# Unread products ahead of the first Gram matrix and ahead of N, and where chunk 0's and 1's K K^T lies

## The chip, the cores and the metric

The kernel runs on one core of a Trainium2 chip. The metric is the device time of one execution in microseconds (us). The engines are named as in the profile: PE (TensorE, the matrix products), PEld (its weight loads), DVE (VectorE), ACT (ScalarE), POOL (GpSimd) and SP (SyncE, which issues most transfers). Each has its own instruction stream and runs it in order; they meet at semaphores. All data are float32.

## The reference

The first half is a delta rule over 32 pairs of batch and head (4 batches, 8 heads, sequence 768, head size 48). For every step t, with k normalised:

```
y[t]  = q[t] @ state
v_old = k[t] @ state
state = state + beta[t] * outer(k[t], v[t] - v_old)
```

Its output, laid out as 3072 tokens by 384, goes through a feed-forward block with an inner size of 1536:

```
g   = x @ w_gate
out = (g * sigmoid(g) * (x @ w_val)) @ w_out
```

## The kernel before

The sequence is cut into 12 chunks of 64 steps. Inside a chunk the recurrence is solved in matrix form: K K^T of the chunk (the Gram matrix), a triangular inverse built from it and from beta, and products with v, q and the state. The 16 slots of a partition are ordered by `par`, the parity of the head, and by two more indices; a batch half and a parity decide which 64 partitions a block uses. The feed-forward block works on 256 tokens, those of one chunk, at a time.

Chunks 0 and 1 are prepared in a stage of their own, in the first 35 us. The functions that matter:

- `load_k`, `load_q`, `load_v` (L133 to L184) issue the first transfers, on SP and ACT.
- `norms(c)` (L361) computes the norms of k on DVE.
- `unread` (L633) issues 94 products of 32 x 32 with one column, whose result nothing reads. They write the PSUM tile `px` and stand at the head of PE's stream.
- `turned(c, of_q, tag)` (L473) transposes k or q of a chunk on PE, eight blocks of 128 x 128 (L497), and ACT copies them to SBUF (L499 or L501). The tag says where in PSUM: a number names two of the four banks `ffn0` to `ffn3`, a string one of the pairs of banks `px` and `py`.
- `first_gram(c, tag)` (L646) forms the Gram matrix of chunk 0 or 1 in 64 products of 32 columns by 64 or by 2 x 32 (L656, L657). Chunk 0 uses the pair `px`, chunk 1 the pair `py`; one tile holds both parities.
- `first_diag(c, p)` (L660) copies the diagonal 32 x 32 blocks to `mb`, in one ACT instruction of 128 x 512.
- `first_n` (L447) turns norms into their reciprocals on DVE (L449, L451, L453); `first_scale` (L673) multiplies beta by them on POOL (L677 to L679) and scales the diagonals on DVE (L682). Between them DVE transposes the diagonals (L1649).
- `low_copies(c, p)` (L664) copies three strips of 16 columns below the diagonal to `l_sb`, one ACT instruction of 128 x 256 each (L667).
- `first_substitution` (L686) inverts the diagonal blocks on DVE (L698, L704), `first_z` transposes the result (L708) and `spread_z` (L711) writes it out twice on ACT and DVE (L717, L719). This is z.
- `warm(3)` (L640) issues three products of 128 columns by 512 (L644), again unread, in `px`.
- `n_products` (L721) forms N from the strips and z (L728). Then `advance(0)` multiplies z with v (L938) and adds three products with N (L958).

The engines' order is written out by hand: inside `manual_schedule` every engine gets its instructions in program order (L1620 to L1706), so what stands earlier in the text is earlier in each engine's queue. Around the change PE's order is: unread products, transposes and Gram matrix of k of chunk 0, transposes of k of chunk 1, beta's products (L438), Gram matrix of chunk 1, transposes of q of chunk 0 and k of chunk 2, q's product of chunk 0 (L513, banks 2 and 3), transposes of k of chunk 3 and q of chunk 1, the Gram matrices of chunks 2 and 3 (L513, `px` and `py`), q's product of chunk 1, the three long products, N.

After that PE works through the feed-forward products and the remaining chunks, interleaved, until the end (L1708 to L1749).

Of the kernel before, what the change touches and what calls it, by code (L numbers as in the profile page):

```python
# [15 lines left out]
R = 32  # L16
# [4 lines left out]
def kernel(  # L21
# [25 lines left out]
    nc = tc.nc  # L47
# [21 lines left out]
    def ps_pair(name, tag):  # L69

        return psum.tile([128, 2, 512], FP32, name=name, tag=tag, bufs=1)
# [7 lines left out]
    def ps_ffn(shape, name, bank=None):  # L79
        if bank is None:  # L80
            taken.append(name)
            bank = (len(taken) - 1) % 4
        n = 1
        for m in shape[1:]:
            n *= m
        p = ffn_banks[bank][:, 0:n]
        return p if len(shape) == 2 else p.rearrange("p (x n) -> p x n", x=shape[1])
# [54 lines left out]
    def load_k(c, dmas=(nc.sync,)):  # L142
        load_heads(kn_of(c), k, c, dmas)

    def load_q(c):
        load_heads(qpad[c % QB], q, c)
# [163 lines left out]
    half = const.tile([128, R], FP32, name="half")  # L310
# [20 lines left out]
    m_low = const.tile([128, 3], FP32, name="m_low")  # L331
# [14 lines left out]
    def half_of(x):  # L346
        return slice(64 * x, 64 * x + 64)

    def every():
        for bp in range(NB):  # L350
            for j in range(NJ):
                for n, (par, b) in enumerate(ORDER):
                    yield bp, j, par, b, bp == 0 and j == 0
# [3 lines left out]
    def new_n(g):  # L357

        n_t[g] = work.tile([128, 2, HH], FP32, name="n_t")
# [106 lines left out]
    def banks(name, tag):  # L466

        if type(tag) is int:
            return [ps_ffn([128, 512], name, tag + i) for i in range(2)]
        p = ps_pair(name, tag)  # L470
        return [p[:, 0], p[:, 1]]
# [75 lines left out]
    def gram(*args):  # L547
        for _ in gram_steps(*args):
            pass
# [51 lines left out]
    B16 = R // 2  # L601
# [28 lines left out]
        )  # L630
        nc.vector.tensor_scalar_mul(m_low, m_rows[:, 0:3], -1.0)

    def unread():  # L633

        p = ps_pair("p_t", "px")[:, 0]
        for n in range(94):
            q_ = QUADS[n % 4][0]
            nc.tensor.matmul(p[q_, 0:1], half[q_], half[q_, 0:1])

    def warm(count):  # L640

        p = ps_pair("p_t", "px")[:, 0]
        for _ in range(count):
            nc.tensor.matmul(p, ident, kts[0][:, 0:512])  # L644

    def first_gram(c, tag):  # L646

        p_g = ps_pair("p_g", tag)
        p_v = p_g.rearrange("p par (x h i) -> p par x h i", x=2, i=R)
        half_rows = C  # L650
        for bp, j, par, b, _ in every():
            k_v = kt[c][half_of(par), bp, j, b].rearrange("p (x i) -> p x i", x=2)
            h, s_ = NJ * bp + j, b ^ par
            hi, lo = slice(64 * s_, 64 * s_ + R), slice(64 * s_ + R, 64 * s_ + C)
            twice = k_v[:, 0:1].to_broadcast([half_rows, 2, R])
            nc.tensor.matmul(p_v[hi, par, :, h], k_v[:, 0], twice)  # L656
            nc.tensor.matmul(p_v[lo, par, :, h], k_v[:, 1], k_v)  # L657
        return p_v

    def first_diag(c, p):  # L660
        to = first_of["diag"][:, HH * c : HH * c + HH]
        nc.scalar.copy(to.rearrange("p (par h) j -> p par h j", par=2), p[:, :, 1])

    def low_copies(c, p):  # L664
        l_v = l_sb[c].rearrange("p (par h) k -> p par h k", par=2)
        for x in range(3):
            nc.scalar.mul(  # L667
                l_v[:, :, :, B16 * x : B16 * x + B16],
                p[:, :, x // 2, :, B16 * (x % 2) : B16 * (x % 2) + B16],
                m_low[:, x : x + 1],  # L670
            )

    def first_scale(r_b):  # L673
        zb, b = first_of["zb"], beta_b[:, 0]
# [418 lines left out]
    def units(t):  # L1093
        return t.rearrange("p (u n) -> p u n", u=4)
# [74 lines left out]
    p_x, p_w, p_y, p_v = (units(bank) for bank in ffn_banks)  # L1169
# [328 lines left out]
    def steps(kind, *args):  # L1498
        return gens.get((kind, args), (None, 0))[1]
# [120 lines left out]
    with tc.manual_schedule(  # L1620
        engines={
            mybir.EngineType.PE,
            mybir.EngineType.Activation,
            mybir.EngineType.DVE,
            mybir.EngineType.SP,
            mybir.EngineType.Pool,
        }
    ):
        new_n(0)
        load_beta()  # L1630
        first_tiles()
        norms(0)
        norms(1)
        load_q(0)
        load_k(2)
        load_k(3)
        load_q(1)
        load_v(0)
        copy_a = nc.scalar.copy
        unread()  # L1640
        turned(0, False, 0)
        p_g = [first_gram(0, "px")]
        first_diag(0, p_g[0])
        turned(1, False, 2)
        spread_beta(copy_a)
        p_g.append(first_gram(1, "py"))
        first_diag(1, p_g[1])
        r_b = first_n()
        nc.vector.transpose(first_of["mb"][:, 0 : R * R], first_of["flat"])  # L1649
        first_scale(r_b)  # L1650
        for n in range(12):
            stage(n, n - 2 if n > 1 else None)
        load_v(1)
        stage(12, 10)
        stage(13, 11)
        low_copies(0, p_g[0])
        turned(0, True, 0)
        low_copies(1, p_g[1])
        turned(2, False, "px")
        first_q = [gram_steps(0, True, 2)]  # L1660
        next(first_q[0])
        turned(3, False, "py")
        turned(1, True, 0)
        gram(2, False, "px", (copy_a, copy_a))
        gram(3, False, "py", (copy_a, copy_a))
        first_q.append(gram_steps(1, True, 0))
        next(first_q[1])
        for n in (0, 2):
            power_step(n)
        first_substitution()  # L1670
        for n in range(14, 18):
            stage(n, n - 3)
        first_z()
        for n in range(18, 23):
            stage(n, n - 3)
        some, others = slice(0, HH // 2), slice(HH // 2, HH)
        spread_z(0, 1, nc.scalar, some)
        spread_z(0, 0, nc.vector)
        spread_z(0, 1, nc.vector, others)
        scale_v(0)  # L1680
        for steps_of in first_q:
            next(steps_of)
        warm(3)
        new_nt(0, qpad[1].rearrange("p bp h d -> p (bp h d)"))
        zb_1 = work.tile([128, R, R], FP32, name="zb", bufs=1)
        new_nt(1, zb_1.rearrange("p k i -> p (k i)"))
        step("advance", advance, 0)
        for x in range(2):
            spread_z(1, x, nc.scalar)
        for n in (4, 1, 3, 5, 6, 7):  # L1690
            power_step(n)
        for _ in range(6):
            step("advance", advance, 0)
        converts_first(0)
        step("advance", advance, 0)
        converts_first(2)
        p_n = banks("p_n", "px")
        n_products(1, p_n, (0,))
        step("advance", advance, 0)
        converts_first(4)  # L1700
        n_products(1, p_n, (1,))
        converts_first(1, 3)
        converts_first(5)
        scale_v(1)
        for par in range(2):
            n_copy(1, p_n, par)  # L1706

        def chain(at):  # L1708

            step("advance", advance, 0 if steps("advance", 0) < 4 else 1)  # L1710
            converts(1 + (at + 1) % 2)

        pairs = [(c, f) for c in range(2) for f in range(0, 8, 2)]
        pairs += [(c, f) for f in range(8, FT, 2) for c in range(2)]
        for at, (c, f) in enumerate(pairs):
            early = c == 0 and f < 4
            if c == 1 and f == 0:
                finish(1)
                second_inverse.append(invert(1))
                for _ in range(3):  # L1720
                    next(second_inverse[0])
            elif not early:
                point(2)
            need((6, 12, 18, 24, 30, 30)[f // 2])
            gate_val(c, f, fill, at, chain if early else None)
        need(len(pieces))
        for bp in range(NB):
            point(2)
            output(0, bp, fill, (4, 8))
        output(1, 0, fill, (4, 8))  # L1730
        hold.clear()
        first_blocks(True)
        first_blocks(False)
        point(2)
        output(1, 1, fill, range(2, FT, 2))
        finish(2)
        x_sums(2)
        sums_of_w(12)
        for c in range(2, NCH):
            if c > FAST:  # L1740
                begin(c, 0)
            point(c + 1)
            if c == FAST:
                begin(c, 0)
            for r in range(ROUNDS):
                gate_val_fast(c, r, fill)
            output_fast(c, fill)
            finish(c + 1)
            x_sums(c + 1)  # L1749
# [30 lines left out]
```

## Time and profile before

| what | value |
|---|---|
| median of three runs | 702.68 us (701.88, 702.68, 706.95) |
| profiled execution | 704.07 us, of which the span of the profile is 702.4 us |
| mean granted clock of PE over the span | 0.994 |
| PE busy | 97% of the span, 11450 product records |
| DVE, ACT, POOL busy | 67%, 37%, 8% |
| chain that ended last | PE 95%, ACT 2%, issue 1%, DVE 1%, DMA 1% |

How to read the profile: an instruction is named by its line in the kernel, its engine and its operation, with the tiles it writes and reads. A float32 product leaves two records on PE and two weight loads on PEld. A wait is put down to the engine or transfer whose semaphore came last; "issue" means that the engine waited for nothing that the profile shows. The start of a record is counted from the start of the span.

### The profile page before, as it was taken

What the parts mean: (1) busy time and instruction counts of PE and PEld (TensorE: products, weight loads), DVE (VectorE), ACT (ScalarE), POOL (GpSimd) and SP (SyncE); (2) the same over time, 40 slices, a digit from 0 to 9 for tenths busy, and PEclk for the clock granted to TensorE, in tenths of its full rate; (3) what the DMA queues carried; (4) which work ended last, traced back from release to release, by engine and by line L of the source; (5) the groups of instructions that cost most, each with busy time, mean ns of one, the idle gap of its engine ahead of it and who ended that gap; (6) DMA issues with size and microseconds to landing.
All of it is one profiled execution on the core that took longest, in us unless ns stands there. A gap on an engine that the chain in (4) does not pass through costs nothing.

```text
span 702.4 us, 25797 instructions
## 1 busy us (share of the span) xinstructions
PE 684.1 (97%) x11450; PEld 643.0 (92%) x11450; DVE 473.0 (67%) x1103; ACT 259.4 (37%) x542; POOL 54.0 (8%) x62
## 2 busy tenths in 40 slices
PE   6899999999999999999999999999999999999997
PEld 5788888757999989999999999999999999999997
DVE  6786788798899738887468787379844345333342
ACT  4674865214442523244223235232153132142220
POOL 4110031105000120000300000200000000000000
PEclk9999999999999999999999999999999999999999
DMA  8578724017450621365333264143241131221210
GB/s 133 155 183 210 215 85 141 4 37 174 126 108 13 118 69 46 77 130 91 75 84 72 56 133 88 31 117 84 55 107 48 42 84 59 55 62 46 68 46 23
DMA packets 143855, 62.33 MB, mean 89 GB/s; under 512 B 122976, under 2 KB 126048, under 8 KB 143744
## 3 DMA queue, kind: packets, MB, share of 16 engines
q1 hardware_dynamic: 141536, 60.19, 36.3%
q8 instruction: 90, 1.47, 0.8%
q10 hardware_dynamic: 2080, 0.39, 0.4%
q0 software_dynamic: 128, 0.10, 0.1%
q14 instruction: 21, 0.17, 0.1%
HBM read 53.58 MB, written 7.08 MB: 86 GB/s over the span
## 4 chain that ended last, share of the span: by engine, by line
PE 95%; ACT 2%; issue 1%; DVE 1%; DMA 1%; ACTq 0%; DVEq 0%
PE ffn L1174 43%; PE ffn L1380 20%; PE ffn L1270 9%; PE ffn L1297 4%; PE p_g L513 3%; PE p_u L938 2%; PE p_r L899 2%; PE p_s L1006 2%; PE p_y L908 2%; PE p_y L994 1%; PE p_f L1067 1%; PE p_u L958 1%; PE ffn L958 1%; PE ffn L497 1%; PE p_j L876 1%
## 5 line engine op out<-in xcount | busy, mean ns | idle before, releaser
L1174 PE MATMUL ffn<-x_ffn,wg_sb 128*128 128x128 f32 x840 | 128.9, 276 | 0.4 <-ACT x_ffn L1073 0.2
L1174 PE MATMUL ffn<-x_ffn,wv_sb 128*128 128x128 f32 x840 | 128.5, 276 | 0.0
L1174 PEld LDWEIGHTS ffn<-x_ffn,wg_sb 128*128 128x128 f32 x840 | 111.7, 193 | 0.6 <-ACT ffn L1230 0.3
L1174 PEld LDWEIGHTS ffn<-x_ffn,wv_sb 128*128 128x128 f32 x840 | 111.1, 193 | 0.1
L1204 ACT ACTIVATE sil<-ffn 128x256 f32<-128x256 f32 x120 | 46.1, 384 | 133.6 <-PE ffn L1174 125.3
L1380 PE MATMUL ffn<-wo_sb,h_f 128*128 128x192 f32 x480 | 83.4, 327 | 0.0
L1209 DVE TENSOR_TENSOR h_f<-sil,ffn 128x256 f32<-128x256 f32 x120 | 49.6, 418 | 49.5 <-ACT sil L1204 47.2
L1380 PEld LDWEIGHTS ffn<-wo_sb,h_f 128*128 128x128 f32 x480 | 78.1, 190 | 0.4
L1341 DVE TENSOR_TENSOR ffn<-ffn,p_sb 128x512 f32<-128x512 f32 x58 | 40.3, 695 | 44.3 <-ACT ffn L1230 43.2
L1174 PE MATMUL ffn<-x_t,h_f 128*128 128x128 f32 x480 | 61.0, 280 | 0.2 <-ACT ffn L1187 0.2
L1174 PEld LDWEIGHTS ffn<-x_t,h_f 128*128 128x128 f32 x480 | 56.2, 191 | 1.4 <-ACT ffn L1187 0.4
L591 DVE TENSOR_TENSOR zb<-zb,tmp 128x31 f32<-128x31 f32 (+15 forms) x155 | 53.1, 343 | 5.3
L585 DVE TENSOR_TENSOR tmp<-zb,mb 128x31 f32<-128x31 f32 (+15 forms) x155 | 52.7, 340 | 4.0
L807 POOL TENSOR_TENSOR n_b<-mb,half 128x32 f32<-128x32 f32 x5 | 30.0, 6003 | 294.6 <-DVE mb L555 294.6
L1341 DVE TENSOR_TENSOR o_sb<-o_sb,ffn 128x192 f32<-128x192 f32 x49 | 17.2, 352 | 51.2 <-PE ffn L1380 49.1
L1187 ACT COPY ffn<-ffn 128x512 f32<-128x512 f32 x30 | 17.1, 571 | 63.7 <-PE ffn L1174 57.3
L1380 PE MATMUL ffn<-last_k,h_f 128*128 128x192 f32 x200 | 35.9, 327 | 0.0
L1270 PE MATMUL ffn<-x_ffn,wg_sb 128*128 128x256 f32 x144 | 34.4, 385 | 0.0
L1270 PE MATMUL ffn<-x_ffn,wv_sb 128*128 128x256 f32 x144 | 33.8, 382 | 0.0
L1380 PEld LDWEIGHTS ffn<-last_k,h_f 128*128 128x128 f32 x200 | 32.9, 190 | 0.0
L1174 PE MATMUL ffn<-x_ffn,p_sb 128*128 128x128 f32 x216 | 30.9, 287 | 0.0
L1270 PEld LDWEIGHTS ffn<-x_ffn,wg_sb 128*128 128x128 f32 x144 | 26.5, 190 | 4.4 <-DVE wg_sb L304 0.8
(289 smaller groups left out, 1070.0 us busy)
## 6 DMA issues: line engine op xcount, KB each, us to landing
h_f<-w_s SPq DMA_DIRECT2D x60, 256.0 KB, 2.7
p_sb<-w_s SPq DMA_DIRECT2D x27, 256.0 KB, 2.9
vin<-in_v_dram SPq DMA_DIRECT2D x48, 96.0 KB, 3.0
out_dram<-o_sb SPq DMA_DIRECT2D x48, 96.0 KB, 2.2
kn<-in_k_dram SPq DMA_DIRECT2D x20, 192.0 KB, 4.8
zt<-in_moe_w_out_dram SPq DMA_DIRECT2D x6, 384.0 KB, 3.7
qpad<-in_q_dram SPq DMA_DIRECT2D x36, 64.0 KB, 2.9
w_s<-h_f SPq DMA_DIRECT2D x7, 256.0 KB, 4.3
```

Of the source, the lines that this page charges most:

```text
L513: nc.tensor.matmul(p_v[par][half_of(b if of_q else b ^ par), bp, j], kt[c][half_of(par), bp, j, b], xt[half_of(par), bp, j, b],)
L585: nc.vector.tensor_tensor(out=t_v, in0=zb[:, 0 : j + 1, j : j + 1].to_broadcast([128, j + 1, m]), in1=mb[:, j : j + 1, j + 1 : R].to_broad ...
L591: nc.vector.tensor_tensor(out=zb[:, 0 : j + 1, j + 1 : R], in0=zb[:, 0 : j + 1, j + 1 : R], in1=t_v, op=ALU.add,)
L807: nc.gpsimd.tensor_tensor(out=n, in0=mb.rearrange("p j i -> p (j i)")[:, 0 : R * R : R + 1], in1=half, op=ALU.pow,)
L1174: nc.tensor.matmul(p[:, u], w(u), moving, start=start and u == 0, stop=True, skip_group_check=True,)
L1187: nc.scalar.copy(p_y, p_x)
L1204: nc.scalar.activation(sil[:, n].rearrange("p (i n) -> p i n", i=2), p[:, 0:2], ACTF.Silu)
L1209: nc.vector.tensor_tensor(out=h_of(c, f, j), in0=sil[:, n].rearrange("p (i n) -> p i n", i=2), in1=p[:, 2:4], op=ALU.mult,)
L1270: nc.tensor.matmul(ps[name][:, i], w_sb[:, t, (f + i) * 128 : (f + i + 1) * 128], xts[c][:, t], start=(t == 0 and i == 0), stop=(t == KT - 1),
L1297: nc.tensor.matmul(p_o, hs[c, f - f % 2][:, f % 2, bp * 128 : (bp + 1) * 128], wo_sb[:, f], start=(f == 0), stop=(f == FT - 1),)
L1341: nc.vector.tensor_tensor(out=out, in0=a, in1=b, op=ALU.add)
L1380: nc.tensor.matmul(p[x, part], a(f - f % 2)[:, f % 2], b(f), start=not begun and f == 0, stop=f == FH - 1, skip_group_check=True,)
```

## The change

It has three parts, all in the stage of chunks 0 and 1.

First, the unread products. `unread` now issues five products of 32 columns by 512 (the moving operand is one column repeated) in place of 94 small ones. The small products have a function of their own, and 56 of them stand ahead of N, where one long product of `warm` is left of three.

Second, the Gram matrices of chunks 0 and 1 have a tile for each parity (`banks`). For chunk 0 these are the two halves of `px`, as before; chunk 1 moves from `py` to the banks `ffn2` and `ffn3`, in which its k was transposed just before.

Third, the copies out of them. The diagonals are copied by parity: for chunk 0 both on ACT, for chunk 1 one on ACT and one on DVE. DVE's copy stands ahead of `first_n` in DVE's order. `low_copies` issues six ACT instructions of 128 x 128 instead of three of 128 x 256.

```diff
-    def unread():
+    def unread(count):
 
         p = ps_pair("p_t", "px")[:, 0]
-        for n in range(94):
+        for _ in range(count):
+            nc.tensor.matmul(p[0:R], half, half[:, 0:1].to_broadcast([128, 512]))
+
+    def small_unread(count):
+
+        p = ps_pair("p_t", "px")[:, 0]
+        for n in range(count):
             q_ = QUADS[n % 4][0]
             nc.tensor.matmul(p[q_, 0:1], half[q_], half[q_, 0:1])
...
     def first_gram(c, tag):
 
-        p_g = ps_pair("p_g", tag)
-        p_v = p_g.rearrange("p par (x h i) -> p par x h i", x=2, i=R)
+        p_v = [p.rearrange("p (x h i) -> p x h i", x=2, i=R) for p in banks("p_g", tag)]
...
-            nc.tensor.matmul(p_v[hi, par, :, h], k_v[:, 0], twice)
-            nc.tensor.matmul(p_v[lo, par, :, h], k_v[:, 1], k_v)
+            nc.tensor.matmul(p_v[par][hi, :, h], k_v[:, 0], twice)
+            nc.tensor.matmul(p_v[par][lo, :, h], k_v[:, 1], k_v)
         return p_v
 
     def first_diag(c, p):
         to = first_of["diag"][:, HH * c : HH * c + HH]
-        nc.scalar.copy(to.rearrange("p (par h) j -> p par h j", par=2), p[:, :, 1])
+        to = to.rearrange("p (par h) j -> p par h j", par=2)
+        nc.scalar.copy(to[:, 0], p[0][:, 1])
+        if c == 0:
+            nc.scalar.copy(to[:, 1], p[1][:, 1])
+        else:
+            nc.vector.tensor_copy(to[:, 1], p[1][:, 1])
 
     def low_copies(c, p):
         l_v = l_sb[c].rearrange("p (par h) k -> p par h k", par=2)
-        for x in range(3):
-            nc.scalar.mul(
-                l_v[:, :, :, B16 * x : B16 * x + B16],
-                p[:, :, x // 2, :, B16 * (x % 2) : B16 * (x % 2) + B16],
-                m_low[:, x : x + 1],
-            )
+        for par in range(2):
+            for x in range(3):
+                nc.scalar.mul(
+                    l_v[:, par, :, B16 * x : B16 * x + B16],
+                    p[par][:, x // 2, :, B16 * (x % 2) : B16 * (x % 2) + B16],
+                    m_low[:, x : x + 1],
+                )
...
-        unread()
+        unread(5)
...
-        p_g.append(first_gram(1, "py"))
+        p_g.append(first_gram(1, 2))
...
-        warm(3)
+        small_unread(56)
+        warm(1)
```

## The prediction

> **What bounds the kernel now.** I read the engine totals first, then PE's list of waits, then the timelines of PE, ACT and DVE over the first 36 us, where all of the change lies, and last the groups of the transposes.
>
> ```profile
> PE 684.1 (97%) x11450; PEld 643.0 (92%) x11450; DVE 473.0 (67%) x1103; ACT 259.4 (37%) x542; POOL 54.0 (8%) x62
> ...
> q8 instruction: 90, 1.47, 0.8%
> ```
> ```profile
> PE ffn L497 <- DVE wo_sb L1649: 2.6, 1, 2.6
> PE p_j L876 <- issue: 2.4, 2, 1.6
> PE ffn L513 <- issue: 1.9, 1, 1.9
> ...
> PE p_y L908 <- issue: 1.2, 1, 1.2
> ...
> PE p_g L656 <- issue: 0.5, 1, 0.5
> ```
> ```profile
> 1.03 2.98 PE L638 MATMUL p_t<-half 32*32 32x1 f32 x188 [1.03 <-DVE half L311]
> ...
> 17.55 1.03 PE L497 MATMUL ffn<-ident,qpad 128*128 128x128 f32 x8 [2.63 <-DVE wo_sb L1649]
> ...
> 28.38 0.80 PE L513 MATMUL ffn<-qt,kt 64*64 64x64 f32 x35 [1.90 <-issue]
> 29.11 2.84 PE L644 MATMUL p_t<-kt,ident 128*128 128x512 f32 x6
> 31.88 1.16 PE L728 MATMUL p_n<-zt,a_sb 64*64 64x64 f32 x64
> ```
> ```profile
> 15.06 1.02 ACT L662 COPY mb<-p_g 128x512 f32<-128x512 f32 x1 [1.93 <-PE p_g L657]
> 15.89 1.20 ACT L667 ACTIVATE a_sb<-p_g,m_low 128x256 f32<-128x256 f32 x3
> ```
> ```profile
> 14.71 0.21 DVE L453 STREAM_TRANSPOSE r_b<-r_n 128x32 f32<-128x32 f32 x1
> 16.11 1.25 DVE L1649 STREAM_TRANSPOSE wo_sb<-mb 128x1024 f32<-128x1024 f32 x1 [1.19 <-ACT mb L662]
> ...
> 28.19 1.03 DVE L719 TENSOR_SCALAR zt<-mb,m_rows 128x512 f32<-128x512 f32 x2
> ```
> ```profile
> L497 PE MATMUL ffn<-ident,kn x16: 367/421/473, 5.7 to 11.5; 128*128 128x128 f32 x16
> L497 PE MATMUL ffn<-ident,qpad x8: 269/272/273, 17.5 to 18.3; 128*128 128x128 f32 x8
> ```
> PE is busy 97% of the span, so what delays PE early comes out at the end. Its waits named "issue" have no releaser; the one put down to DVE L1649 is of the same kind, since that transpose of chunk 0's q reads nothing DVE wrote after 6.9 us. They have a pattern. A product is four PE records (94 products, 188 matmul records and as many loads), a transpose two. Counted so, PE stops at record 704 (third of chunk 1's Gram matrix), 960 (third of q's transposes), 1472 (middle of L513) and 2752 (second of p_y): all are 192 + 256n. The instruction queue moved 90 packets of 16.4 KB for 23,000 records, one per 256. So PE waits for its own instructions. Entering a block starts the next one's fetch: 8.29 to 13.33, 13.33 to 17.55 and 24.34 to 28.38 are 5.0, 4.2 and 4.0 us from entry to the next block; the fetch after 33.12 was there after 3.1.
>
> The other thing to see: z is ready at 29.2 (L719), N's products (L728) start at 31.88. DVE's chain has 2.7 us of slack; PE's stream sets N.
>
> [...]transposes take 421 ns up to 11.5 us and 272 later; the first clock record, full speed, is at 11.7.[...]
>
> **The change, part by part.** Times are in the profiled execution (span 702.4, run 704.07, which is 1.4 over the median of 702.68).
>
> *Five long products for 94 small ones.* L644's three took 2.84, so 0.92 each at full clock and, estimated, 1.84 at half. All start cold at 1.03.[...] They then end at 6.5 to 8.2; I take 7.4[...]. k landed at 5.57, so chunk 0's transposes start 1.7 late, but run warm (1.03 for eight, not 1.94), and its Gram products end near 10.5, not 10.02. The records before them drop from 376 to 20, so block 192 now begins 154 records into this Gram matrix, entered near 9.4; the next (448) begins 103 records into chunk 1's, at 9.4 + 4.4 = 13.8. PE waits for it there, then 153 records at 1.71/256 each: end 14.85, against 15.04. Ends: 13.9 and 16.3.
>
> *Diagonals by two engines.* One ACT copy of 512 took 1.02; the halves take about 0.55 on ACT and 0.45 on DVE (0.35 to 0.6), side by side. But DVE's copy stands ahead of first_n's three instructions (14.11 to 14.92, 0.81), which were done while PE worked; POOL's scaling and the transpose L1649 queue behind them. L1649 starts at 14.85 + 0.45 + 0.85 = 16.15 against 16.11: the split buys nothing on this chain. POOL's work (15.07 to 16.05 for nb, 0.15 behind r_b) ends near 17.3 and hides under L1649 (to 17.4). z comes at 29.3, within N's slack; without that slack it would count fully.
>
> *low_copies in six.* Three at 0.40 become six at about 0.27 (0.22 to 0.3; 512-element ACT copies repeat every 0.54, 256 every 0.33 to 0.40): +0.4 per chunk on ACT. Chunk 0's q products write banks 2 and 3, where chunk 1's Gram now lies, so they wait for all six; queued behind them on PE are the transposes of chunks 3 and 1 (chunk 3's need no longer wait for chunk 1's Gram, which has left their tile) and the Gram matrices of 2 and 3. q's transposes no longer stop at 960 (start 14.9, not 17.55), and ACT goes on without a gap: 14.85 + 0.55 + 1.6 + 1.1 + 1.6 = 19.7, products at 19.8 against 20.16. Of the 2.6 us removed 0.4 is left, as ACT is late next. A tile per parity releases nothing early: the products alternate parities. No DMA is added or moved on SP's or POOL's queue.
>
> *56 small and one long ahead of N.* The stream from 20.16 to 25.95 repeats 0.4 earlier (slow clock around 18.5 to 21.9 as before, an assumption). Block 960 begins 160 records into the Gram pair of chunks 2 and 3 (256 records, 23.92 to 25.95): 23.5 + 1.3 = 24.8. Block 1216 begins 30 records into the small products, at 24.8 + 4.2 = 29.0; PE is there at 26.9 and waits. Then 194 records at 2.98/376 = 1.5, the long one 0.9: N at 31.5, 0.4 earlier. But N's 57th record opens block 1472, due at 29.0 + 4.2 = 33.2; N reaches it at 32.0, waits 1.2 and ends at 33.8, where it ended at 33.0: **+0.8**. Block 1728 begins 55 records into the first product with N (L958, before at 34.62, now 35.4): due 33.2 + 3.1 = 36.3, reached 35.8: **+0.5**. Bounds of the two together: -1.5 (every fetch 3.1) to +3 (5.0).
>
> *The rest of the stream.* From N on the instructions are the same, 356 - 216 = 140 records earlier against the blocks. The stops of before after N sum to 5.8 us: 1.4 near 50, 1.3 from 161 to 170, 2.0 at 245 and 250, 1.0 at 349. Taking the trace's own pace with its stops taken out, and 4.2 us a fetch[...]: near 50 the stretch from p_r to p_u is again 3.6 us long and the stop stays; about 1.3 stays from 157 to 165; at 245, 250 and 349 nearly all goes, some 1.1 comes near 254 to 353 and 531: **-1.9** (-4 to +1). After the stop at 250 the clock was at half for 3.4 us (250.6 to 254.0), worth up to 1.6; I take **-0.4**.
>
> Sum: 0.8 + 0.5 - 1.9 - 0.4 = -1.0: 701.4 for the span, **701.7** against the median.
>
> **Rivals.** *Slower: the blocks of N come late.* One mechanism: two fetches in a row, 1216 and 1472, under the weight transfers. At 5.0 each (as from 8.29) N's second half starts at 34.8 and L958 follows, 1.9 later than above plus the same 1.3; the later stops give back nothing: 702.7 + 3.2 = 705.9. For it: those fetches run beside 100 to 300 GB/s. Against: 4.0 to 4.3 measured between 17 and 32. Above 4.9 us a fetch the sum turns positive even with most of the later gain. *Slower: the long products don't lift the clock.* 9.2 us, end 10.2; Gram 0 and with it everything 3 to 4 later: 706.5. Against: products of 64 columns did lift it. *Faster: short fetches.* 3.1 each, no wait in N (-1.5), later stops and the slow window mostly gone (-2.5): 698.7. For it: 2.8 to 3.1 after 33; against: 4 before it. *It doesn't do what it says* holds in part, and is in the forecast: warm start and split copy end in waits for instructions and ACT.
>
> **How the numbers follow.** Forecast 0.5 (700 to 703.5), late blocks 0.22, cold products 0.1, short fetches 0.18. The range 698.4 to 706.6 leaves out the outer third of the late blocks (0.07), half of the cold products (0.05) and 0.07 of the short fetches. One per cent, 7 us, is about what a measurement of this kernel can tell from no change (its runs span 701.88 to 706.95). No case reaches it alone; I leave 0.02 for faster, 0.04 for slower.
>
> **What would show it.** Right: the L638-type row is five products ending at 6.5 to 8.2; chunk 0's transposes near 272 ns; no stop of PE before q's transposes; a stop inside the 56 small products and one some 57 records into N; DVE's copy ahead of first_n; fewer "issue" waits after 240. Wrong: N starting before 30.5, stops elsewhere than at 192 + 256n, or a slow clock through chunks 2 and 3, which would add 2 to 3.

## The result, and the profile after

The changed kernel takes 699.45 us (median of 8 runs, 695.95 to 700.46) beside 703.3 for the kernel before (8 runs, 701.35 to 706.95): ratio 0.9946, 95% interval 0.9924 to 0.9969. That is 3.85 us faster, where 1.0 was forecast; it stays within 1%. The profiled executions take 699.69 and 704.07, spans 698.0 and 702.4, so they differ by 4.4.

The page's engine line and the instruction queue of the changed kernel:

```profile
PE 684.8 (98%) x11380; PEld 638.7 (92%) x11380; DVE 473.1 (68%) x1104; ACT 259.8 (37%) x549; POOL 54.6 (8%) x62
...
q8 instruction: 89, 1.46, 0.9%
```

35 products fewer, 70 product records and 70 loads, one block less (89 packets of the instruction queue, 90 before). PE is not busy for less time (684.8 against 684.1, long products and slow clock included); it waits less. Its waits:

```profile
PE p_t L644 <- issue: 1.2, 1, 1.2
PE ffn L662 <- issue: 1.1, 1, 1.1
PE p_t L497 <- POOL beta_b L688: 1.1, 1, 1.1
PE p_t L637 <- DVE half L311: 1.0, 1, 1.0
PE p_y L919 <- issue: 0.7, 1, 0.7
```

The three largest of before are gone: the 2.6 ahead of q's transposes, the 2.4 in p_j (near 250 and 349), the 1.9 in q's product. Two of the new ones were forecast: one in the small products (L644), one in chunk 1's Gram matrix (L662). The one put down to POOL ends just after ACT's six copies out of `px` do (17.82), so chunk 2's transposes, which write `px`, most likely wait for ACT. PE's timeline over the front, without the rows of the two Gram matrices:

```profile
1.03 7.08 PE L637 MATMUL p_t<-half 128*32 128x512 f32 x10 [1.03 <-DVE half L311]
8.04 1.09 PE L497 MATMUL ffn<-ident,kn 128*128 128x128 f32 x8
...
15.69 1.09 PE L497 MATMUL ffn<-ident,qpad 128*128 128x128 f32 x8
17.91 1.07 PE L497 MATMUL p_t<-ident,kn 128*128 128x128 f32 x8 [1.13 <-POOL beta_b L688]
19.62 0.32 PE L513 MATMUL ffn<-qt,kt 64*64 64x64 f32 x2 [0.64 <-DVE zt L715]
20.39 1.98 PE L513 MATMUL ffn<-qt,kt 64*64 64x64 f32 x62 [0.45 <-ACT a_sb L678]
...
27.65 0.29 PE L644 MATMUL p_t<-half 32*32 32x1 f32 x14
29.15 0.97 PE L644 MATMUL p_t<-half 32*32 32x1 f32 x98 [1.20 <-issue]
30.21 2.07 PE L650 MATMUL p_t<-kt,ident 128*128 128x512 f32 x2
32.22 1.78 PE L739 MATMUL p_n<-zt,a_sb 64*64 64x64 f32 x62
```

The long products end at 8.1 and chunk 0's transposes take 1.09 for eight, 273 ns each (421 before). Nothing of that arrives at N: it starts at 32.22, where it started at 31.88. L650 takes 2.07 for one long product, where one took 0.92 at full clock, and the trace's clock record is at half from 30.19 to 33.60. ACT and DVE between the two Gram matrices and the inverse:

```profile
15.76 0.61 ACT L668 COPY mb<-ffn 128x256 f32<-128x256 f32 x1 [2.62 <-PE ffn L662]
16.17 1.65 ACT L678 ACTIVATE a_sb<-p_g,m_low 128x128 f32<-128x128 f32 x6
```
```profile
15.89 0.61 DVE L672 COPY mb<-ffn 128x256 f32<-128x256 f32 x1 [2.12 <-PE ffn L662]
...
17.08 1.20 DVE L1660 STREAM_TRANSPOSE wo_sb<-mb 128x1024 f32<-128x1024 f32 x1
...
29.14 1.04 DVE L730 TENSOR_SCALAR zt<-mb,m_rows 128x512 f32<-128x512 f32 x2
```

DVE's copy takes 0.61, and the transpose of the diagonals follows at 17.08 instead of 16.11.

Where the time went, by PE's busy time in stretches (columns: stretch in us from the start, its length, PE busy, records, granted clock, DMA share, GB/s). Before, then after:

```profile
31.90:45.00 13.10, 12.44 (x456) 1.00 0.50 141
45.00:60.00 15.00, 13.81 (x350) 1.00 0.83 209
...
240.00:260.00 20.00, 18.39 (x489) 0.91 0.34 75
...
340.00:360.00 20.00, 19.14 (x507) 1.00 0.40 90
```
```profile
31.90:45.00 13.10, 11.82 (x413) 0.94 0.47 138
45.00:60.00 15.00, 15.00 (x391) 1.00 0.80 193
...
240.00:260.00 20.00, 20.00 (x520) 1.00 0.41 91
...
340.00:360.00 20.00, 20.00 (x457) 1.00 0.39 88
```

At 245 to 250 and at 349 neither kernel has anything that the change touches, and there PE's gaps are gone and the clock is full. Matching each PE record from N on with the same one of before, the changed kernel is 0.3 behind at N, 2.4 behind at 45, 0.8 behind at 51, 1.8 behind at 163, 0.3 behind at 170, 1.7 ahead at 250, 3.3 ahead at 254, 4.4 ahead at 350 and at the end. So the front costs 2.4, and 6.8 come back later.

### The profile page after: what moved, and what is told of

It reads as the page before. It is cut to its first block, busy times and chain, and to the rows that moved or that the text cites. A ratio compares the mean times of both kernels' runs of the same rounds, so it can differ in the third digit from the quotient of the medians.

```text
span 698.0 us, 25668 instructions
## 1 busy us (share of the span) xinstructions
PE 684.8 (98%) x11380; PEld 638.7 (92%) x11380; DVE 473.1 (68%) x1104; ACT 259.8 (37%) x549; POOL 54.6 (8%) x62
## 4 chain that ended last, share of the span: by engine, by line
PE 94%; DVE 3%; ACT 1%; issue 1%; DVEq 0%; ACTq 0%
PE ffn L1185 43%; PE ffn L1391 20%; PE ffn L1281 9%; PE ffn L1308 4%; PE p_g L513 2%; PE p_s L1017 2%; PE p_u L949 2%; PE p_r L910 2%; PE p_y L919 2%; PE p_y L1005 1%; PE p_t L637 1%; PE ffn L969 1%; PE p_u L969 1%; PE p_f L1078 1%; PE p_j L873 1%
## 5 line engine op out<-in xcount | busy, mean ns | idle before, releaser
L1185 PEld LDWEIGHTS ffn<-x_ffn,wv_sb 128*128 128x128 f32 x840 | 110.7, 192 | 0.0
L1281 PE MATMUL ffn<-x_ffn,wv_sb 128*128 128x256 f32 x144 | 33.8, 382 | 0.0
L1281 PEld LDWEIGHTS ffn<-x_ffn,wv_sb 128*128 128x128 f32 x144 | 27.0, 190 | 3.7
```

What stands on the lines that cost most here:

```text
L1185: nc.tensor.matmul(p[:, u], w(u), moving, start=start and u == 0, stop=True, skip_group_check=True,)
L1281: nc.tensor.matmul(ps[name][:, i], w_sb[:, t, (f + i) * 128 : (f + i + 1) * 128], xts[c][:, t], start=(t == 0 and i == 0), stop=(t == KT - 1),
```

## The experiments

One table for all, by the records of PE. *Recorded order* counts everything that PE's queue left in the trace, from 0: loads, products and semaphore records; the prediction's 192 + 256n are the same edges, counted one lower. *Shift* is how many records earlier against the blocks of 256 the stream from N on lies than in the kernel before; a whole block counts as none. *Stops* are the gaps of more than 0.12 us at an edge 193 + 256n of the recorded order which ended within 1.2 to 1.8 us after a fetch had landed. A gap runs from the start of one record to the start of the next, so it holds some 0.2 us that are not idle: of the 6.0 of before PE is idle for 4.5, of the 2.7 of the changed kernel for 1.5. *Half clock* counts the time after N's start in which the clock record is at half, without the last microseconds (in the trace of before it falls to half at 701.2, behind PE's work). *N to end* runs from N's first record to the last one. The last four columns are from one profiled execution.

| kernel | ratio of times, 95% | shift | N starts | stops from N on | half clock | N to end |
|---|---|---|---|---|---|---|
| before | 1 | 0 | 31.9 | 6.0 | 3.4 | 670.4 |
| changed | 0.9946 (0.9924 to 0.9969) | 140 | 32.2 | 2.7 | 1.4 | 665.7 |
| 59 at the head | 0.9910 (0.9891 to 0.9929) | 140 | 29.1 | 1.1 | 0 | 666.1 |
| changed, 91 ahead of N | 1.0071 (1.0047 to 1.0095) | 0 | 38.1 | 6.6 | 3.0 | 670.3 |
| changed, small head | 0.9944 (0.9922 to 0.9966) | 140 | 28.9 | 3.8 | 6.8 | 669.5 |
| changed, not split | 0.9939 (0.9916 to 0.9962) | 140 | 30.4 | 3.4 | 10.2 | 669.7 |
| 51 at the head | 0.9918 (0.9895 to 0.9941) | 172 | 28.9 | 2.1 | 0 | 666.6 |
| 87 at the head | 0.9991 (0.9979 to 1.0004) | 28 | 29.7 | 8.7 | 0 | 671.1 |
| 123 at the head | 0.9970 (0.9960 to 0.9980) | 140 | 34.0 | 1.9 | 6.8 | 667.2 |
| 59 at the head, split | 0.9929 (0.9901 to 0.9956) | 140 | 30.1 | 2.4 | 0 | 664.6 |
| changed, wide 56 | 0.9942 (0.9921 to 0.9962) | 140 | 31.9 | 2.7 | 0 | 665.1 |
| none at the head | 0.9928 (0.9911 to 0.9945) | 120 | 28.5 | 3.1 | 3.4 | 667.1 |

*N to end* still holds the slow clock, which falls differently in each execution. As an estimate, half of the *half clock* time is lost (from the changed kernel's one long product at half clock, 2.07, and the 0.92 that one took at full clock). Without it the last column goes by the shift: 668.7 and 668.8 at shift 0, 671.1 at 28, 663.8 to 666.1 in the seven kernels at 140, 665.4 at 120, 666.6 at 172.

The theory: what pays is where the edges of the instruction blocks fall after N; the warm start, the split and the small products ahead of N buy nothing of their own that can be measured. The rival: something in those three parts pays.

**The edges alone.** The kernel before with 59 small products, which removes the same 140 records and changes nothing else.

```diff
-        for n in range(94):
+        for n in range(59):
```

> The kernel before, with 59 small unread products at its head in place of 94 and nothing else changed. From N on its instructions then stand against the blocks of 256 exactly where they stand in the changed kernel. Theory (PE waits for blocks of its own instructions; what the change moved is 140 records): the stops of PE at 50, 245, 250 and 349 us go, the half clock after 250 too; ahead of N no stop is left behind chunk 1's Gram matrix, N starts near 29.6 with a warm clock; about 7 us less than before, near 696.5 (694.5 to 699), so faster than the changed kernel. Rival (the long products, the split copies or the 56 and one ahead of N earn the gain): none of them is here, so 702 to 703.5.

696.79 (694.31 to 697.4) beside 702.52 (701.01 to 703.95). The stretch from N to the end is 4.3 shorter than before, and PE's gaps at 245 to 250 and 349 are gone in the same way:

```profile
240.00:260.00 20.00, 20.00 (x481) 1.00 0.37 83
340.00:360.00 20.00, 20.00 (x458) 1.00 0.44 94
```

So the gain needs none of the change's parts; 35 small products less are enough, and with them N comes 3.1 earlier than in the changed kernel. One thing was not as expected: ahead of N, where no stop was to be left, there is one of 1.7 at 24.0, in chunk 3's Gram matrix.

**The change without the edges.** 91 instead of 56 small products ahead of N give back the 140 records.

```diff
-        small_unread(56)
+        small_unread(91)
```

> The changed kernel with 91 small products ahead of N in place of 56: 35 more, 140 records, so that from N on the instructions stand against the blocks as in the kernel before; all else as changed. Theory (instruction blocks): the stops at 50, 245, 250 and 349 come back, about 4.5 us, and N starts 1.5 to 3 later; near 706 (703.5 to 708). Rival (warm start, copies): only the 35 products' own 1.1 us are added, 700.5.

707.24 (706.15 to 711.01): all parts of the change at the old edges are slower than before. The stops of before are back, at the same products (recorded edges 2753, 5825, 8897, 12481), and N to end is 670.3, as before. PE's waits:

```profile
PE p_t L644 <- issue: 3.7, 2, 2.2
PE p_j L887 <- issue: 2.0, 2, 1.2
...
PE p_y L919 <- issue: 0.9, 1, 0.9
```

The front is worse than expected: N starts 5.9 later than in the changed kernel, not 1.5 to 3. Two edges, not one, fall into the small products (the 3.7 of L644), and the clock is at half from 20.7 to 27.5 and from 34.4 to 41.2. That profiled execution took 710.21, 3 more than the median, so part of this is its own.

**Without the warm start.** Five small products in place of five long ones.

```diff
-        unread(5)
+        small_unread(5)
```

> The changed kernel with five small unread products at its head in place of the five long ones: the same number of records, so no block moves, but PE is free at 5.6 us and cold. Theory (instruction blocks and PE's stream set N; the warm start is eaten by the long products' own end at 8.0): chunk 0's transposes take 421 ns again, its Gram matrix ends near 10.0 to 10.3, chunk 1's some 0.5 earlier than in the changed kernel; within 1 of it, 698.7 likeliest. Rival (the warm start earns part of the gain): 700.5 to 702.

698.72 (696.12 to 700.95), ratio 0.9944 beside the changed kernel's 0.9946. The warm start can't be told from none. In the profiled execution N comes earlier (28.9), but then the clock is at half for 6.8.

**Without the split.** The changed kernel with `first_gram`, `first_diag` and `low_copies` of before, chunk 1 in `py` again.

```diff
-        p_v = [p.rearrange("p (x h i) -> p x h i", x=2, i=R) for p in banks("p_g", tag)]
+        p_g = ps_pair("p_g", tag)
+        p_v = p_g.rearrange("p par (x h i) -> p par x h i", x=2, i=R)
...
-        p_g.append(first_gram(1, 2))
+        p_g.append(first_gram(1, "py"))
```

> The changed kernel with the Gram matrices, the diagonal copies and the strip copies as before (one tile for both parities, chunk 1 in py, one ACT copy of the diagonals, three strips); the products at the head and ahead of N as changed, every record at its place. Theory: the split bought nothing: chunk 1's diagonals reach the transpose some 0.3 earlier, ACT is 0.5 earlier with the strips; 699.0 (698 to 700). Rival (the split copies shorten the chain to z and so earn part of the gain): 700 to 701.5.

698.09 (696.23 to 701.85), ratio 0.9939: no gain from the split can be told either. Whether it costs something is asked again below.

**More records gone, or a better place?** 51 at the head.

```diff
-        for n in range(94):
+        for n in range(51):
```

> The kernel before with 51 small products at the head instead of 94 (59 gave 696.8). Against the blocks everything from N on is now 172 records earlier than before, not 140. Blocks theory: the stops left in the 59 version after N (1.1 us at 40, 157, 161 and 377) go too, since the stretches that eat a block in under 4 us no longer lie right behind an edge; N stays at 29.1, where z (not PE) sets it: 696.0 (694.5 to 697.5), with no stop from 155 to 170 in the trace. Rival, that fewer records as such are what pays: 8 products less are 0.25 us at most and they end before k has landed, so 696.8, and the stops at 157 to 165 stay.

Ratio 0.9918, which both allowed. The trace decides against my sum: no stop from 155 to 170, as expected, but new ones at 46.5 (0.96), 52.1 (0.33) and 363.5 (0.34) and two small ones at 67.9 and 171.1; 2.1 in all, more than the 1.1 with 59. A fixed time for a fetch names the bad places, not the best one.

**A bad place, with less work.** 87 at the head.

```diff
-        for n in range(94):
+        for n in range(87):
```

> The kernel before with 87 small products at the head instead of 94: 28 records less, so less work. Blocks theory: this is close to the worst place for the edges; the stops after N grow from 5.8 us to about 7.7, nothing is given back, and the kernel is slower with less work: 704.3 (703 to 706). Rival, that the later gain comes from fewer instructions or from a calmer start and not from where the edges fall: 702.3 or a little less, as the kernel before.

The ratio is 0.9991 (0.9979 to 1.0004): not slower, so the forecast failed, and the time is the one that the rival gave. The later part held all the same: 8.7 of stops from N on where 7.7 were expected and 6.0 are in the kernel before. What I had left out is the front: with 28 records less the stop of 2.7 ahead of q's transposes became one of 0.2, and N came 2.2 earlier. Against 59 at the head the comparison is clean, because the clock is full in both traces from 10 us until the last few: 28 small products more, N 0.6 later, the end 5.6 later; the ratios differ by 0.0081, which is 5.7 us. PE's waits with 87:

```profile
PE p_y L908 <- issue: 2.6, 2, 2.1
PE p_u L938 <- issue: 2.2, 2, 1.6
...
PE p_j L876 <- issue: 1.3, 2, 0.9
```

**A whole block more.** 123 at the head: 59 and 64 more, 256 records.

```diff
-        for n in range(94):
+        for n in range(123):
```

> The kernel before with 123 small products at the head instead of 94, which is the 59 version plus 64 products, 256 records: one whole block more, so all edges from the Gram matrices on fall where they fall with 59. Blocks theory: the head now runs over an edge at about 4.7 and stops for the next block until about 7, so everything up to N is some 1.7 later than with 59; the later gain is that of 59 in full: 698.5 (697 to 701), faster than before with 29 more products. Rival, that fewer products are what pays: 702.5 plus 29 x 0.03 and more, 703.4 to 706.

0.9970 (0.9960 to 0.9980), so faster than before with 29 more products; the later gain is there (1.9 of stops from N on). The front is worse than expected, N at 34.0: the stop inside the head lasted 3.8, and the clock was full only from 21.4 on.

```profile
1.03 3.44 PE L638 MATMUL p_t<-half 32*32 32x1 f32 x223 [1.03 <-DVE half L311]
8.30 0.49 PE L638 MATMUL p_t<-half 32*32 32x1 f32 x23 [3.83 <-issue]
```

**The split at the fast head.** 59 small products and three long ones, with the split tile and copies.

```diff
-        unread(5)
+        small_unread(59)
...
-        small_unread(56)
-        warm(1)
+        warm(3)
```

> The changed kernel with 59 small products at the head instead of five long ones, and three long products ahead of N instead of 56 small and one long: the 59 version of the kernel before (696.8) with only the split tile, the two-engine copy and the six low copies added. Theory: DVE's copy delays the transpose of the Gram rows by 0.6 us (17.08 against 16.45 in the changed kernel without the split), z comes 0.6 later and N waits for it: 697.5 (696.8 to 698.5). Rival, that the split costs nothing: 696.8. Rival, that the whole 1.9 us by which N came earlier without the split was the split's: 698.7.

Ratio 0.9929 (0.9901 to 0.9956) beside 0.9910 (0.9891 to 0.9929): the intervals overlap, and a price of the split can't be told from the times. In the traces DVE's transpose starts at 15.84 instead of 15.21, as expected, and N, which waits for z in both, at 30.1 instead of 29.1.

**The slow clock at N.** The 56 products made 64 columns wide.

```diff
-            nc.tensor.matmul(p[q_, 0:1], half[q_], half[q_, 0:1])
+            nc.tensor.matmul(p[q_, 0:64], half[q_], half[q_, 0:1].to_broadcast([32, 64]))
```

> The changed kernel with the 56 small products ahead of N made 64 columns wide instead of one: the same number of records at the same places against the blocks, but work for the array as in the Gram matrices. In the changed kernel the clock fell to half from 30.2 to 33.6, after a window whose products other than the small ones took 0.94 us of 3.41. Theory: [...]with wide ones (some 2.0 us in place of 1.7) [...]the clock stays full through N, and 0.3 more work is paid for 1.7 less: 698.0 (697 to 699.2) where the changed kernel has 699.45, and no half clock from 28 to 37. Rival, that the stop of 1.4 us inside them lowers the clock whatever they are: half clock again, 699.8.

No half clock from 18.5 on, as the theory wanted, and N to end is 665.1. But the ratio, 0.9942 (0.9921 to 0.9962), is that of the changed kernel, so it can't tell the two numbers apart. One execution can't settle the cause: where the clock's windows lie differs between executions, as the last section shows.

**Nothing at the head.** The kernel before without the call.

```diff
-        unread()
```

> The kernel before without any product at its head: 94 less, 376 records, so from N on the edges fall where 120 records less would put them. Blocks theory: a place a little worse than that of 59 (the stretches of fast blocks at 157 to 170 and at 250 start nearer behind an edge, my sum of later stops is 0.8 us higher), and the head's products end before k has landed anyway, so nothing else is saved: 697.6 (696.5 to 699.5). Rival, that fewer records as such are what pays: 236 less than with 59, better than its 696.8: 695 to 696.

697.18 beside 701.69, ratio 0.9928 (0.9911 to 0.9945), which is 697.4 on the scale of the first runs' 702.5, beside the 697.6 of the blocks theory; the rival's 695 to 696 (0.989 to 0.991) lie below the interval. 236 records less than with 59, and not faster.

The best version is the kernel before with 59 small products, 0.9910; 51, none at the head, and 59 with the split can't be told from it. Its own interval and the changed kernel's overlap by little (0.9924 to 0.9929).

## Why the prediction was right, and where its sizes were off

The sign, the class and the mechanism held: PE waits for its own instructions, the front gives nothing, and the gain comes hundreds of microseconds later from edges moved by 140 records. The forecast was -1.0 and the median moved by -3.85. The terms missed in opposite directions, the front by +1.1 and the later stops and the clock by -4.5 together, so the sum is nearer than its later part alone, and that much is luck. In the prediction's own steps:

*Five long products: right, at the late end.* They end at 8.1 (7.4 taken, 6.5 to 8.2 expected), transposes at 273 ns in place of 421, the stop inside chunk 1's Gram matrix is there. What was wrong is the clock's rise, an estimate of mine that the trace of before doesn't show: the changed kernel's first clock record, full, is at 6.29, behind 3.41 us full of long products (2.88 to 6.29), and the 1.85 us of them up to 2.88 had not lifted it. The stop came 0.9 later than forecast (the block after 192 was entered at 10.1, not 9.4, and the next was there 4.6 later, not 4.4), so that matrix ended at 15.7 instead of 14.85.

*Diagonals: right.* The copy's record is 0.61 long, but DVE's next instruction starts 0.46 after it (15.89 to 16.35), where 0.45 was forecast, an estimate of mine: before has no DVE copy of 256 elements (its rows L1048 and L1071, 354 ns for 192 and 550 for 384, would put it at 0.42, an estimate too). The transpose came 0.97 later than before, not 0.04; of the 0.93 between, the Gram matrix's later end makes 0.85. z was still ready before PE needed it.

*low_copies: right about who is late, too early by 0.6.* One product of q starts at 19.62 (19.8 forecast), but the other 31 only at 20.39, when ACT is done with the second bank; before, they started at 20.16. With the slow clock at 19.95 to 23.36, PE reached the edge in the small products at 27.95, not 26.9. It cost little, since the block behind that edge was there at 29.15 only (29.0 forecast).

*Ahead of N: +0.8 and +0.5 forecast, +2.4 measured at 45.* The stop in the small products is there. The stop of 1.2 some 57 records into N is not. The clock fell to half from 30.2 to 33.6: the long product took 2.07 instead of 0.9, N started at 32.2 instead of 31.5 and ran slowly, and it ends at 34.1 all the same (33.8 forecast). A slow clock there was no step of the forecast. L969 starts at 35.62 (35.4), its stop is 0.71 (0.5), and two more edges, at 40.9 and 44.7, add 0.58.

*The rest of the stream: the step that was mis-sized.* -1.9 was forecast. From 45 on the records gain 6.8; without the 1.6 of the clock that is -5.2, of which the listed stops give 4.6 (6.0 before, 1.4 after); the other 0.6 is spread over 45 to 60 and 163 to 170 in steps of some 0.2. What stays from 157 to 165 was right (1.26, forecast 1.3), and so was that 245, 250 and 349 go. Two things were wrong. The stop at 50 was to stay and is gone: in the changed kernel the fetch that serves this stretch moves at 51.03, 0.35 ahead of the edge at 51.38; before, it moved at 48.48, 1.88 after the edge. Why it moved earlier was not shown. I had given every fetch 4.2 us. And the 1.1 expected near 254, 353 and 531 did not come: behind 165 the table's sum has one gap of 0.16, at 380, in which PE is not idle.

*The clock at 250: -0.4 forecast, -1.6 in the trace.* I had taken a quarter of it. It went whole between these two executions; how often a run of the kernel before has it was not measured.

The front's +2.4, the later stops' -5.2 and the clock's -1.6 make the trace's -4.4. The rival of short fetches had the nearest time (698.7) and part of its reason: no wait in N, later stops mostly gone. Its 3.1 us for every fetch was not met (3.3 to 4.6 at the stops of the changed kernel). "It doesn't do what it says" held fully: the small head and the unsplit copies do no worse.

## What to carry to other kernels

When PE's stream is the bound and a wait has no releaser, count its records (here four to a float32 product, two to a transpose, and its semaphore records) and see whether the gaps fall at a fixed distance (here 256). If they do, removing or adding a few unread products at the head moves every later edge, and may be worth more than the edit that it comes with (here 0.9910 with 59 at the head, 0.9946 with the whole change); test any edit of PE's stream against a version with the same number of records removed elsewhere. Keep stretches of tiny products, which use up a block in less than 4 us, off the place right behind an edge (at the stops here the next block was there 3.3 to 5.9 us after one), and choose by measuring a few counts: the sum told bad from good, not good from best.

## What the runs showed of the hardware

**The cost of instruction blocks.** The stops, counted over the whole trace as in the table, are 11.9 us of 702 before and 5.4 after (9.5 and 3.8 of them idle), and the delay isn't one number. At the stops of over 0.2 us in the traces of before, the changed kernel, 59 and 123, the next block was there 3.3 to 4.2 us after an edge where its packet began within 1.4 us of that edge, and 4.4 to 5.9 where it began over 2 us behind it. What delays the start was not tried.

**The clock's windows.** In the trace of before the clock record changes at 11.69, 18.51, 21.93, 250.62 and 254.03, in that of the changed kernel at 6.29, 19.95, 23.36, 30.19 and 33.60: in each, neighbours lie a whole number of steps of 3.413 us apart (1 to 67 of them). Such a step is called a window here. The grid's position differs from trace to trace: in four kernels with the same five long products at the head, window edges fall at 2.88, 0.22, 3.13 and 1.39 us. Two drops of the kernel before, with the window ahead of each (columns as above):

```profile
15.10:18.51 3.41, 0.96 (x9) 1.00 0.90 154
18.51:21.93 3.42, 3.42 (x73) 0.50 0.74 138
247.20:250.60 3.40, 1.84 (x133) 1.00 0.04 11
250.60:254.00 3.40, 3.40 (x17) 0.50 0.17 51
```

PE was busy for 0.96 of 3.41 us ahead of the first drop and for 1.84 of 3.40 ahead of the second. Where a drop follows a stop, it costs up to 1.7 more (an estimate: half of the 3.4 us at half clock). Not every stop was followed by one: with 91 small products the stop at the same edge as the second drop's, 1.4 long, lay in a window (256.22 to 259.64) in which PE was busy for 2.17, and the clock stayed full. Whether the grid's position in an execution decides that was not shown. A single profile therefore shows one draw of the slow clock, and the difference of two profiles should be read with its clock windows taken apart.

**Transposes and the clock.** With 51 at the head PE was busy for 2.25 us of the window from 14.16 to 17.57, 2.16 of it with transposes, and the clock, full before, stayed full. With 91 ahead of N the clock rose from half at 27.53; in the window before, PE was busy throughout, for 2.83 us with transposes. The first line is all of PE, the second its transposes alone, the third the window after:

```profile
24.12:27.53 3.41, 3.41 (x38) 0.50 0.57 172
24.12:27.53 3.41, 2.83 (x14) 0.50 0.57 172
27.53:30.94 3.41, 2.88 (x194) 1.00 0.62 189
```

In the same trace 2.61 us of long products in the window up to 3.64 did not raise it. So the prediction's reading, that products of 64 columns had lifted the clock, is not borne out: in the trace of before PE was busy for 3.39 and 3.42 us of the two windows that end at 11.69 and 21.93, with the transposes counted. Busy time alone is not the measure either: with 123 at the head one-column products filled 3.31 of the window from 0.93 to 4.34, and the clock was full only from 21.4 on. What lifts the clock stays open.
